# A prompt block with multi-query attention and a GELU layer on one core: when small VectorE work is issued

## The chip, the cores and the metric

The kernel runs on one core of a Trainium2 chip. The metric is device time in microseconds (us). The core's engines each run their own queue of instructions in order: TensorE (PE; its weight loads are listed apart as PEld), VectorE (DVE), ScalarE (ACT), GpSimd (POOL) and SyncE (SP), which issues the transfers.

## The reference

The input x has 2048 rows of 512 numbers, in fp32. A modulation vector is made of `c` and `w_mod` (six parts: shift, scale and gate for either half). The first half is attention, the second a GELU layer:

```
h = layernorm(x) * (1 + ca) + sa
q = h @ wq            # 32 heads of 16; k = h @ wk and v = h @ wv are shared by all heads
p = softmax(q k^T / 4)
x = x + ga * (concat_heads(p @ v) @ wo)
h = layernorm(x) * (1 + cb) + sb
x = x + gb * (gelu(h @ w1 + b1) @ w2 + b2)     # 1376 hidden numbers, tanh form
```

## The kernel before, in words

The rows are cut into 8 blocks of 256, and a block's 32 heads into 8 groups of 4 heads: 64 units, worked in order. A unit takes 8 steps over the keys, two at a time. Such a pair of steps is the kernel's rhythm. The clock that the planner counts goes up by four in it, and one count is called a tick here (the diff's words call it a half step). A pair has two halves. In each half TensorE makes four score products `e` for this unit (L650, with ScalarE's exponentials `p`, L658), four products `m` for a later unit whose row maxima VectorE takes (L527, L532), and the products of the exponentials with the values, `acc` (L675), of a step that lies behind. The products `m` share three PSUM banks.

Beside this runs the rest of the block before: output projection, second norm, GELU layer. Its products come in batches, one per pair, each cut in two halves by rows of the array (`half`, L208). A batch is taken from a queue of generators at the start of a pair. All smaller work is put off by `later(n, fn)`: `fn` is called n ticks on, and then issues its instructions on whichever engines they use, behind what stands there. So a tick sets a place in each engine's order, not a time. `due()` runs the calls whose tick has come, in the order in which they were put off: before the pair, between its halves (two ticks), and behind the second half. The order of TensorE's work follows from the generators, which ask for the tick and for what has been issued.

When a unit ends, `finish_unit` copies its sums (`oc`, L687) and sends them to memory one tick later. For blocks 5, 6 and 7 (`EARLY`) the softmax sums are then fetched as a tile of 64 x 16 (L712), inverted by VectorE (`sums`, L715) and stored (`drs`, L716); after every second head group the heads and the spread factors are fetched (`os`, L722 and L724) and GpSimd multiplies them (L728) before the norm's split (`norm_early`). The last two head groups of block 7 take another way.

`rest_steps` makes the output projection of a block in two row groups of 128 rows, t = 0 and 1. Each ends with `add_x` on VectorE (`x`, L853), bn_stats on two halves of the row (`st`, L860), and, for both groups together, bn_aggr on VectorE (`mv`, L867), four small GpSimd instructions (`ve`, `rs`, `nm`, L868 to L873) and the normed rows on GpSimd (`xh`, L880). Eight ticks after the projection TensorE may turn the normed rows (`tp`, L976 in the code, recorded at L208). Blocks 4 and 5 hold back the last 12 products of their second output sum (`w2ps`) until the next block's projection is through, so that TensorE has them during these eight ticks; the next blocks, 5 and 6, are the two that the diff's second part touches. That sum ends with `ot` on VectorE (L1083). Units 48 to 55 belong to block 6 and carry block 5's rest; units 56 to 63 carry block 6's.

Of the kernel before, what the change touches and what calls it, by code (L numbers as in the profile page):

```python
# [44 lines left out]
TAIL = (14, 9, 7)  # L45
EARLY = 5
HELD = 4
LATER = 4
LONE = 5
SOON = 6  # L50
# [13 lines left out]
def adaln_mqa_mlp(  # L64
# [24 lines left out]
    NQ = H // 4  # L89
# [67 lines left out]
    def later(n, fn):  # L157
        if draining[0]:
            fn()
        else:  # L160
            pending.append((clock[0] + n, fn))
# [518 lines left out]
    def finish_unit(u):  # L680
        b, Q = units[u]
        w = blocks[b][1]
        acc = accs.pop(u)
        if len(ocs) < 2:
            ocs.append(att.tile([P, w], F32, name=f"oc{u}", tag="oc", bufs=2))
        oc = ocs[u % 2]
        ins = nc.scalar.copy(oc, acc)  # L687
        if u - 2 in copied:
            tc.declare_no_dep(ins.ins, copied[u - 2], reason="the transfer that reads the tile's last contents comes between the two")
        copied[u] = ins.ins.name  # L690

        def send_o():
            nc.sync.dma_start(out=do[b][Q].rearrange("c r n -> (c r) n"), in_=oc)

        final = b == len(blocks) - 1
        if final and Q >= NQ - 2:
            if Q == NQ - 2:
                assert stage[b - 1] == 1
                later(2, lambda: fetch_rest(b))
                later(5, lambda: norm_early(b, range(KD - 1)))  # L700
            return
        later(1, send_o)
        if b < EARLY:
            return
        g = Q // 2
        if Q == 0:
            heads_of[b] = att.tile([P, 2, KD, w], F32, name=f"os{b}", tag="opk", bufs=1)
        os_ = heads_of[b]
        sums = wts_pool["rest"].tile([4 * w // 16, 16], F32, name=f"sums{u}", tag="sums", bufs=2)

        def fetch_sums():
            nc.sync.dma_start(out=sums, in_=do[b][Q:Q + 1, :, 16, :].rearrange("q c (t n) -> (q c) t n", n=16))  # L712

        def invert_sums():
            nc.vector.reciprocal(out=sums, in_=sums)  # L715
            nc.sync.dma_start(out=drs[b][4 * Q:4 * Q + 4, :].rearrange("h (t n) -> (h t) n", n=16), in_=sums)  # L716
            if Q % 2:
                collect()

        def collect():  # L720
            src = do[b][2 * g:2 * g + 2, :, 0:16, :].rearrange("q c r n -> (q c) r n")
            nc.sync.dma_start(out=os_[:, 0, g, :], in_=src)  # L722
            src = drs[b][8 * g:8 * g + 8, :].unsqueeze(1).to_broadcast([8, 16, w])
            nc.sync.dma_start(out=os_[:, 1, g, :], in_=src)  # L724
            later(3 if Q == NQ - 1 else 4, scale_heads)

        def scale_heads():
            nc.gpsimd.tensor_tensor(out=os_[:, 0, g, :], in0=os_[:, 0, g, :], in1=os_[:, 1, g, :], op=ALU.mult)  # L728
            if Q == NQ - 1:
                norm_early(b, [g])  # L730

        later(3, fetch_sums)
        later(4 if Q == NQ - 1 else 6, invert_sums)
        if Q == NQ - 2:
            later(5, lambda: norm_early(b, range(KD - 1)))

# [14 lines left out]
    def rest(b, fast):  # L751
# [58 lines left out]
        if b >= EARLY:  # L810
            ons[0] = on_early[b][0]
            ready[0] = clock[0] + HELD
        else:
# [19 lines left out]
    def rest_steps(b, fast, rp, bank, ons, ready):  # L833
# [4 lines left out]
        for hf in range(w // HQ):  # L838
# [20 lines left out]
            def stats(t, h):  # L859
                nc.vector.bn_stats(out=st[:, t, h, :], in_=x1[:, t, h * D // 2:(h + 1) * D // 2])  # L860
# [4 lines left out]
            def rstd(t0, t1):  # L865
                for t in range(t0, t1):
                    nc.vector.bn_aggr(out=mv[:, t, :], in_=st[:, t].rearrange("p h n -> p (h n)"))  # L867
                (nc.vector if fast else nc.gpsimd).tensor_scalar(out=ve[:, t0:t1], in0=mv[:, t0:t1, 1], scalar1=EPS,  # L868
                                                                 scalar2=0.0, op0=ALU.add, op1=ALU.add)
                nc.gpsimd.tensor_tensor(out=rs[:, t0:t1], in0=ve[:, t0:t1], in1=mhalf[:, t0:t1], op=ALU.pow)  # L870
                if not fast:
                    nc.gpsimd.tensor_tensor(out=nm[:, t0:t1], in0=mv[:, t0:t1, 0], in1=rs[:, t0:t1], op=ALU.mult)
                    nc.gpsimd.tensor_scalar(out=nm[:, t0:t1], in0=nm[:, t0:t1], scalar1=-1.0, scalar2=0.0, op0=ALU.mult, op1=ALU.add)  # L873

            def xhat(t):
                if fast:
                    nc.vector.tensor_scalar(out=xh[:, t, :], in0=x1[:, t, :], scalar1=mv[:, t, 0:1], scalar2=rs[:, t:t + 1],
                                            op0=ALU.subtract, op1=ALU.mult)
                else:
                    nc.gpsimd.tensor_scalar(out=xh[:, t, :], in0=x1[:, t, :], scalar1=rs[:, t:t + 1], scalar2=nm[:, t:t + 1],  # L880
                                            op0=ALU.mult, op1=ALU.add)
# [8 lines left out]
            def out_sum(t):  # L890
                return psum.tile([P, D], F32, name=f"wops{b}_{hf}_{t}", **bank())
# [7 lines left out]
            if fast:  # L899
                turned = [psum.tile([P, HQ], F32, name=f"turned{q}", **bank()) for q in range(2)]  # L900
                rows_o = rp.tile([P, HQ], F32, name="rows_o", tag="rb", bufs=2)
                inv = att.tile([P, H * w // P], F32, name="inv", tag="rsum", bufs=1)

                def turn_o(q):
                    for t in range(2):
                        nc.tensor.transpose(turned[q][:, t * P:(t + 1) * P], ocs[q][:, t * P:(t + 1) * P], ident)

                def scale_o(q):
                    src = turned[q].rearrange("p (t c r) -> p t c r", t=2, c=4)
                    by = inv[:, 8 * q:8 * q + 8].rearrange("p (t c) -> p t c", t=2)  # L910
                    dst = rows_o.rearrange("p (t q c r) -> p q t c r", t=2, q=2, c=4)[:, q]
                    nc.vector.reciprocal(out=by, in_=src[:, :, :, 16])
                    for t in range(2):
                        nc.vector.tensor_tensor(out=dst[:, t], in0=src[:, t, :, 0:16],
                                                in1=by[:, t].unsqueeze(2).to_broadcast([P, 4, 16]), op=ALU.mult)

                turn_o(0)
                scale_o(0)
                pss = [out_sum(t) for t in range(2)]
                yield from batches(pss[0], out_pairs(0, [0]), BATCH, end=False)  # L920
                turn_o(1)
                scale_o(1)
                yield from batches(pss[0], out_pairs(0, [1, 2]), BATCH, begin=False, end=False)
                back = psum.tile([P, HQ], F32, name="back", **bank())
                for t in range(2):
                    nc.tensor.transpose(back[:, t * P:(t + 1) * P], rows_o[:, t * P:(t + 1) * P], ident)
                split(onH[:, KD - 1, :], onL[:, KD - 1, :], back, nc.scalar, nc.vector)
                yield from batches(pss[1], out_pairs(1, [0]), BATCH, end=False)
                yield from batches(pss[0], out_pairs(0, [KD - 1]), BATCH, begin=False)
                add_out(0, pss[0])  # L930
                yield from batches(pss[1], out_pairs(1, range(1, KD)), BATCH, begin=False)
                add_out(1, pss[1])
                for t in range(2):
                    xhat(t)
            else:
                for t in range(2):
                    ps = out_sum(t)
                    yield from batches(ps, out_pairs(t, range(KD)), BATCH, lambda g: b < EARLY or g in on_early[b][1])
                    add_x(t, ps)

                    for h in range(2):
                        later(3 - 2 * t + 2 * h, lambda t=t, h=h: stats(t, h))
                projected.add(b)
            if not fast:
                later(4, lambda: rstd(0, 2))
                later(5, lambda: xhat(0))
                later(5, lambda: xhat(1))
                later(9, lambda: add_bias(0))
                later(9, lambda: add_bias(1))

                later(BUSY, lambda: state.update(busy=True))
                yield 8
# [167 lines left out]
            elif held_back:  # L1120
                yield from second(0, range(NF))
                yield from second(1, range(NF - LATER), put=add_x)
                while b + 1 not in projected:
# [525 lines left out]
```

## Time and profile before

| | |
|---|---|
| median of 3 runs | 1547.63 us (1547.52 to 1547.88) |
| the profiled execution | 1547.75 us, its span 1545.9 us |
| TensorE busy | 1531.1 us, 99% |
| VectorE busy | 1393.6 us, 90% |
| ScalarE busy | 1227.3 us, 79% |
| GpSimd busy | 671.9 us, 43% |
| granted TensorE clock | full in all 40 slices |

The busy time of TensorE is that of pipelined products, so 99% does not mean that it is at its peak. The 22 reciprocals of the softmax sums lie between 998.5 and 1468.5 us; the projection of block 5 with its norm lies around 1166 to 1206 us, that of block 6 around 1333 to 1376 us.

### The profile page before, as it was taken

How to read it: one execution, taken by the hardware profiler on the slowest of the kernel's cores; microseconds unless marked ns; L12 is line 12 of the kernel's file. 1: busy time of each engine (PE TensorE's matmuls, PEld its weight loads, DVE VectorE, ACT ScalarE, POOL GpSimd, SP SyncE). 2: the span in 40 equal slices, each digit the busy share in tenths (PEclk: the TensorE clock that was granted, in tenths of full speed). 3: DMA queues.
4: the chain of work that ended last, by engine and by line, in shares of the span. 5: the costliest groups of instructions: out<-in, count | busy, mean ns of one | idle time of the engine just before them, and what ended most of it. 6: DMA issues, size and time to landing. Idle time of an engine off the chain costs nothing.

```text
span 1545.9 us, 41617 instructions
## 1 busy us (share of the span) xinstructions
PE 1531.1 (99%) x16421; PEld 953.9 (62%) x16421; DVE 1393.6 (90%) x2487; ACT 1227.3 (79%) x2401; POOL 671.9 (43%) x1229
## 2 busy tenths in 40 slices
PE   7999999999999999999999999999999999999999
PEld 4555555567655665557655676556655676566668
DVE  7999999999999999999999999999999999999914
ACT  5677887788778887788877887788877888778874
POOL 7545422887323570246522462235711574046511
PEclk9999999999999999999999999999999999999999
DMA  9145312422030211213012120303112220203141
GB/s 294 52 138 186 118 46 79 135 74 87 23 107 17 87 57 36 94 30 99 30 56 76 56 87 23 105 25 100 57 31 73 67 96 25 88 28 98 49 151 49
DMA packets 84203, 120.85 MB, mean 78 GB/s; under 512 B 21330, under 2 KB 57426, under 8 KB 83752
## 3 DMA queue, kind: packets, MB, share of 16 engines
q1 hardware_dynamic: 84008, 118.19, 23.7%
q8 instruction: 130, 2.13, 0.6%
q14 instruction: 65, 0.53, 0.1%
HBM read 90.87 MB, written 26.74 MB: 76 GB/s over the span
## 4 chain that ended last, share of the span: by engine, by line
PE 81%; DVE 9%; issue 4%; POOL 2%; SPq 1%; DMA 1%; ACT 0%; POOLq 0%; DVEq 0%; ACTq 0%
PE acc L675 28%; PE m L527 22%; PE e L650 15%; DVE mx L532 8%; PE w1ps L208 8%; PE w2ps L208 3%; PE w2ps L197 1%; PE w1ps L197 1%; PE wops L208 1%; PE tp L208 1%; PE qps L208 1%; DMA wqf<-in_A_wq_dram 1%; SPq L498 0%; DVE st L860 0%; POOL qL L149 0%
## 5 line engine op out<-in xcount | busy, mean ns | idle before, releaser
L532 DVE TENSOR_REDUCE mx<-m 128x1 f32<-128x512 f32 x2048 | 1270.1, 682 | 82.7 <-PE m L527 59.1
L658 ACT ACTIVATE p<-e 128x512 f32<-128x512 f32 x2048 | 1097.6, 598 | 251.6 <-PE e L650 114.3
L527 PE MATMUL m<-ks,qst 64*128 64x512 f32 x2048 | 838.8, 430 | 2.1 <-DMA qst<-dq 0.7
L650 PE MATMUL e<-qst,ks 64*128 64x512 f32 x2048 | 748.9, 412 | 0.0
L675 PE MATMUL acc<-p,va 128*32 128x256 f32 x8192 | 546.8, 385 | 0.0
L527 PEld LDWEIGHTS m<-ks,qst 64*128 64x128 f32 x2048 | 367.8, 184 | 213.8 <-DVE mx L532 182.7
L650 PEld LDWEIGHTS e<-qst,ks 64*128 64x128 f32 x2048 | 363.1, 184 | 75.1 <-ACT p L658 53.4
L675 PEld LDWEIGHTS acc<-p,va 128*32 128x32 f32 x8192 | 214.5, 109 | 213.3 <-issue 108.9
L208 PE MATMUL w1ps<-h2H,w1t 64*128 64x256 f32 x1232 | 235.0, 287 | 0.0
L588 POOL TENSOR_SCALAR mt<-turned 8x32 f32<-8x32 f32 x252 | 52.7, 209 | 410.2 <-DVE turned L594 398.1
L208 PEld LDWEIGHTS w1ps<-h2H,w1t 64*128 64x128 f32 x1232 | 185.6, 184 | 29.1 <-DVE mx L532 18.5
L208 PE MATMUL w1ps<-h2L,w1t 64*128 64x256 f32 x616 | 168.9, 274 | 0.0
L208 PE MATMUL w2ps<-w2H,gH 64*128 64x512 f32 x288 | 127.1, 441 | 0.2
L208 PEld LDWEIGHTS w1ps<-h2L,w1t 64*128 64x128 f32 x616 | 113.7, 185 | 0.0
L208 PE MATMUL w2ps<-w2L,gH 64*128 64x512 f32 x288 | 112.8, 392 | 0.0
L208 PE MATMUL w2ps<-w2H,gL 64*128 64x512 f32 x288 | 112.3, 390 | 0.0
L1020 POOL TENSOR_SCALAR tt<-tt 128x256 f32<-128x256 f32 x77 | 31.2, 406 | 122.8 <-ACT tt L1019 91.4
L208 PEld LDWEIGHTS w2ps<-w2H,gH 64*128 64x128 f32 x288 | 52.9, 184 | 13.0 <-issue 2.9
L1021 POOL TENSOR_TENSOR tt<-tt,z 128x256 f32<-128x256 f32 x77 | 56.9, 739 | 6.4
L149 POOL TENSOR_TENSOR gL<-z,gH 128x256 fp32r<-128x256 f32 x77 | 56.8, 738 | 6.4
L1031 POOL TENSOR_TENSOR z<-tt,z 128x256 f32<-128x256 f32 x77 | 56.6, 735 | 6.0
L1030 POOL TENSOR_TENSOR tt<-tt,z 128x256 f32<-128x256 f32 x77 | 56.6, 735 | 0.0
(199 smaller groups left out, 1474.2 us busy)
## 6 DMA issues: line engine op xcount, KB each, us to landing
w1t<-dw SPq DMA_DIRECT2D x82, 512.0 KB
qst<-dq SPq DMA_DIRECT2D x384, 32.0 KB
do<-oc SPq DMA_DIRECT2D x62, 128.0 KB
dw<-w1s SPq DMA_DIRECT2D x11, 512.0 KB
xt<-in_A_x_dram SPq DMA_DIRECT2D x4, 1024.0 KB
dq<-qH SPq DMA_DIRECT2D x16, 256.0 KB
dq<-qL SPq DMA_DIRECT2D x16, 256.0 KB
x<-in_A_x_dram SPq DMA_DIRECT2D x8, 512.0 KB
```

The lines of the kernel that those rows point to most:

```text
L149: eng_l.tensor_tensor(out=dst_l, in0=src, in1=raw(dst_h), op=ALU.subtract)
L208: ins = nc.tensor.matmul(ps, a[rows], b_[rows], start=first_ and turn == 0, stop=last_ and turn == 1)
L527: nc.tensor.matmul(m, qsts[u][rows, j, t * P:(t + 1) * P], ks[rows, kc * 512:(kc + 1) * 512], start=True, stop=True)
L532: nc.vector.tensor_reduce(out=self.mx[u][:, i, kc:kc + 1], in_=m, axis=AX.X, op=ALU.max)
L588: nc.gpsimd.tensor_scalar(out=mt[:, g:g + 32], in0=turned[g:g + 4 * T, :], scalar1=1.0, scalar2=0.0, op0=ALU.mult, op1=ALU.add)
L650: nc.tensor.matmul(e, ks[rows, kt * P:(kt + 1) * P], rhs, start=True, stop=True)
L658: ins = nc.scalar.activation(dst, e, AF.Exp, scale=0.25)
L675: ins = nc.tensor.matmul(accs[u][32 * cidx:32 * cidx + 32, :], va[:, kt, :], rhs, start=kt == 0, stop=kt == NKT - 1)
L1020: nc.gpsimd.tensor_scalar(out=tt, in0=tt, scalar1=1.0, scalar2=1.0, op0=ALU.mult, op1=ALU.add)
L1021: nc.gpsimd.tensor_tensor(out=tt, in0=tt, in1=z, op=ALU.mult)
L1030: nc.gpsimd.tensor_tensor(out=tt, in0=tt, in1=z, op=ALU.mult)
L1031: nc.gpsimd.tensor_tensor(out=z, in0=tt, in1=z, op=ALU.add)
```

## The change

The reciprocals of the softmax sums, with all that hangs on them (store, fetch of heads and factors, GpSimd's product four ticks later), are issued ten ticks after the unit's end instead of six, except those of a block's last head group. In blocks 5 and 6 the bn_stats of the second row group are issued two ticks later, bn_aggr with GpSimd's small instructions two ticks later, and the normed rows one tick later, at the same tick as bn_aggr.

```diff
+INVERT = 10
...
         later(3, fetch_sums)
-        later(4 if Q == NQ - 1 else 6, invert_sums)
+        later(4 if Q == NQ - 1 else INVERT, invert_sums)
...
                     for h in range(2):
-                        later(3 - 2 * t + 2 * h, lambda t=t, h=h: stats(t, h))
+                        later(3 - 2 * t + 2 * h + (2 if b >= EARLY and t else 0), lambda t=t, h=h: stats(t, h))
                 projected.add(b)
             if not fast:
-                later(4, lambda: rstd(0, 2))
-                later(5, lambda: xhat(0))
-                later(5, lambda: xhat(1))
+                later(6 if b >= EARLY else 4, lambda: rstd(0, 2))
+                later(6 if b >= EARLY else 5, lambda: xhat(0))
+                later(6 if b >= EARLY else 5, lambda: xhat(1))
```

## Rows read from the trace of the kernel before

**Rows 1.** The page: busy us of each engine; a GpSimd group of the GELU.
```profile
PE 1531.1 (99%) x16421; PEld 953.9 (62%) x16421; DVE 1393.6 (90%) x2487; ACT 1227.3 (79%) x2401; POOL 671.9 (43%) x1229
...
L1031 POOL TENSOR_TENSOR z<-tt,z 128x256 f32<-128x256 f32 x77 | 56.6, 735 | 6.0
```
**Rows 2.** Waits before weight loads: total us, times, longest.
```profile
PEld m L527 <- DVE mx L532: 182.7, 468, 1.0
```
**Rows 3.** The reciprocals by tile `sums`: shortest, median, longest ns; first, last start.
```profile
L715 DVE RECIPROCAL sums<-sums x22: 233/234/245, 998.5 to 1468.5; 64x16 f32<-64x16 f32 x22
```
**Rows 4.** Half pairs of block 5's projection: length; busy us by engine, clock, DMA.
```profile
1176.75:1179.71 2.96, 2.96 (x33) 1.78 (x31) 2.96 (x6) 2.19 (x5) 0.69 (x2) 1.00 0.00 0
...
1188.22:1191.39 3.17, 3.17 (x32) 1.85 (x30) 3.17 (x6) 2.38 (x6) 0.00 (x0) 1.00 0.00 0
1191.39:1194.32 2.93, 2.93 (x31) 1.78 (x31) 2.93 (x8) 2.34 (x5) 0.86 (x2) 1.00 0.14 48
1194.32:1197.16 2.84, 2.84 (x31) 1.65 (x30) 2.62 (x6) 2.16 (x4) 2.01 (x5) 1.00 0.02 1
...
1200.01:1203.01 3.00, 2.90 (x35) 1.83 (x33) 3.00 (x6) 2.52 (x6) 2.92 (x4) 1.00 0.00 0
1203.01:1205.72 2.71, 2.71 (x35) 1.76 (x33) 2.48 (x5) 1.88 (x5) 0.23 (x1) 1.00 0.33 84
```
**Rows 5.** VectorE's time line there: start us, us, instruction, count.
```profile
1188.12 0.68 DVE L853 TENSOR_TENSOR x<-wops,x 128x512 f32<-128x512 f32 x1
...
1189.91 0.42 DVE L860 BATCH_NORM_STATS2 st<-x 128x6 f32<-128x256 f32 x1
1190.25 2.47 DVE L532 TENSOR_REDUCE mx<-m 128x1 f32<-128x512 f32 x4
1192.63 0.42 DVE L860 BATCH_NORM_STATS2 st<-x 128x6 f32<-128x256 f32 x1
...
1193.21 2.43 DVE L532 TENSOR_REDUCE mx<-m 128x1 f32<-128x512 f32 x4
...
1199.94 0.69 DVE L1083 TENSOR_TENSOR ot<-w2ps,x 128x512 f32<-128x512 f32 x1
```
**Rows 6.** TensorE's weight loads: the fourth maximum product of the half pair from 1188.22.
```profile
1190.97 0.18 PEld L527 LDWEIGHTS m<-ks,qst 64*128 64x128 f32 x1
```
**Rows 7.** Half pairs of block 6's projection, as rows 4.
```profile
1358.25:1361.53 3.28, 3.28 (x33) 1.86 (x31) 3.28 (x7) 2.51 (x6) 0.68 (x2) 1.00 0.02 4
1361.53:1364.46 2.93, 2.93 (x32) 1.80 (x31) 2.93 (x8) 1.84 (x4) 0.87 (x2) 1.00 0.01 3
...
1370.14:1373.03 2.89, 2.89 (x34) 1.83 (x32) 2.89 (x5) 2.41 (x6) 0.00 (x0) 1.00 0.23 91
```
**Rows 8.** Half pairs behind `ot`: with a reciprocal (unit 41), without (unit 17).
```profile
996.76:999.74 2.98, 2.98 (x32) 1.83 (x30) 2.98 (x6) 2.20 (x6) 0.69 (x2) 1.00 0.86 324
...
456.88:459.76 2.88, 2.88 (x32) 1.75 (x30) 2.88 (x5) 2.17 (x5) 0.68 (x2) 1.00 0.56 224
```
**Rows 9.** VectorE's time line at a reciprocal in a GELU stretch; idle time in brackets.
```profile
1450.56 0.23 DVE L715 RECIPROCAL sums<-sums 64x16 f32<-64x16 f32 x1
1450.72 2.41 DVE L532 TENSOR_REDUCE mx<-m 128x1 f32<-128x512 f32 x4
1453.43 2.48 DVE L532 TENSOR_REDUCE mx<-m 128x1 f32<-128x512 f32 x4 [0.30 <-PE m L527]
```
**Rows 10.** GpSimd's time line in block 5: first of the chain, normed rows.
```profile
1193.38 0.23 POOL L868 TENSOR_SCALAR ve<-mv 128x2 f32<-128x2 f32 x1 [15.85 <-DVE mv L867]
...
1195.07 1.53 POOL L880 TENSOR_SCALAR xh<-x,rs,nm 128x512 f32<-128x512 f32 x2
```
**Rows 11.** TensorE's first weight load for turning block 5's normed rows.
```profile
1201.31 0.18 PEld L208 LDWEIGHTS tp<-ident,xh 64*128 64x128 f32 x1
```
**Rows 12.** Waits of the SyncE queue and of GpSimd: total us, times, longest.
```profile
SPq L716 <- DVE sums L715: 57.1, 10, 6.7
...
POOL os L728 <- DMA os<-drs: 20.9, 9, 5.5
```

## The prediction, made before the change was timed

> **What bounds the kernel now.** I read the page's busy shares first: TensorE stands at 99% and VectorE at 90% of the span [rows 1], so neither share alone says which of them sets the pace. The waits say where they touch: the largest wait before TensorE's weight loads is for VectorE's maxima, 182.7 us in 468 pieces [rows 2]. Most of these 0.4 us pieces recur in every half pair and cost nothing by themselves, so the next view is the time line cut into half pairs. I cut it at the first weight load of the products with the exponentials (`acc`), which come once per half pair. An undisturbed half pair with extra products takes 2.84 to 2.85 us [the row from 1194.32 in rows 4]. It holds four maxima, which take 2.41 us from start to start of what follows (2.48 us for the merged row less the overlap, [rows 9]). So VectorE has 0.43 us to spare per half pair and TensorE paces. The half pairs that are longer than 2.85 us all have VectorE busy for their whole length: 2.96, 3.17, 2.93 and 3.00 us in block 5's projection [rows 4], 3.28 and 2.93 us in block 6's [rows 7], and 2.98 us behind an output sum with a reciprocal after it [rows 8]. These are the places where VectorE paces, and the change moves VectorE's instructions out of some of them.
>
> The mechanism is seen in [rows 5, 6]. The maxima have three PSUM banks, so the fourth maximum product of a half pair waits for the first reduction. In the half pair from 1188.22 the sum `x` ran late in the one before, a bn_stats stands in front, and the first reduction starts at 1190.25, that is 2.03 us in. The fourth product's load comes at 1190.97, 0.72 us later. The half pair is 0.33 us too long. In the next one the reduction starts 1.82 us in (1193.21) and the loss is 0.09 us. Both give one threshold: a first reduction up to about 1.73 us into the half pair costs nothing, and every later 0.1 us costs 0.1 us.
>
> **The change part by part.** *Reciprocals.* Of 22 reciprocals [rows 3], 20 move by four ticks, one pair of steps; the two after the last head group of blocks 5 and 6 stay at four ticks. Each advances VectorE by 0.16 us (1450.56 to 1450.72, [rows 9]). In none of them does VectorE wait for the sums today: they start as the reduction before them ends, and no idle time is listed before any of them. So no DMA wait is removed. What a move is worth depends on what stands in front. Behind a GELU bias or nothing, the following half pairs still have 0.30 us of idle time [rows 9], before and after the move: zero, for 14 of the 20. Two stand behind an output sum `ot`, in units 41 and 55: 2.98 us for the first, where the same place in unit 17, without a reciprocal, took 2.88 us [rows 8]; the new place has no sum in front. Gain 2 x 0.10 = 0.20 us. One stands behind block 4's second sum in a stretch without extra products, where VectorE is busy throughout on both sides of the move: between 0 and 0.16 us, I take 0, since a block of VectorE work stays as long wherever the piece stands in it. The other three are in the two held-back blocks and are counted there.
>
> What follows a reciprocal moves too: the transfer that stores it, for an odd head group the two that fetch heads and factors, and GpSimd's product of them. The SyncE queue is held up by the reciprocal today, up to 6.7 us at a time [rows 12]; behind it stand the rows of maxima, the next query tile and a weight piece. After the change the first two stand ahead of it and go out earlier; a weight piece still has three pairs (17 us) until it is read. GpSimd waits 20.9 us at its nine products [rows 12]; the wait follows the reciprocal at the same four ticks' distance, and GpSimd is 43% busy [rows 1]. In block 5's place it now comes behind both halves of the norm's transposed output instead of between them. I set all this at zero, with a bound of 0.3 us either way. After the maxima have run out (last reciprocal) VectorE is idle: zero.
>
> *Block 5, second row group and norm.* Half pair by half pair, from [rows 4, 5] and the threshold:
> - 1176.75 (2.96): its reciprocal goes, the reduction starts 0.16 us earlier, below the threshold. Gain 0.11.
> - Two half pairs on, the reciprocal joins the first group's second bn_stats: 0.34 + 0.16 us in front, with VectorE free about 1.2 us in; the first reduction starts at about 1.68. Just below the threshold: zero, by 0.05 us.
> - 1188.22 (3.17): no bn_stats any more; the start goes from 2.03 to 1.69. Gain 0.33.
> - 1191.39 (2.93): one bn_stats (0.34) instead of bn_stats and two bn_aggr (0.58, 1192.63 to 1193.21). Start about 1.60. Gain 0.09.
> - 1194.32 (2.84): the other bn_stats and the bn_aggr arrive, 0.58 us. Start about 1.75. Cost 0.02.
> - The next one has the turned maxima in front and the held-back sum `ot` of 0.69 us, as before, but with some 0.2 us of backlog. It still just fits: cost 0.01.
> - 1200.01 (3.00; an undisturbed one with transposes takes 2.71): the reciprocal goes (-0.16), the backlog replaces it (+0.17). Cost 0.01 to 0.02.
> Gain 0.11 + 0.33 + 0.09 - 0.05 = 0.48 us.
>
> *Block 6.* [rows 7] 1358.25 (3.28): reciprocal and bn_stats go, 0.44 gained. 1361.53 (2.93): 0.09 gained. The one after, an ordinary one now, gets bn_stats, reciprocal and bn_aggr together, 0.34 + 0.16 + 0.24 = 0.74 us; the first reduction starts 1.92 us in: cost 0.19. The one with `ot` and its follower stay. Gain 0.34 us.
>
> *The cover of the later norm.* Against the transposes, bn_aggr ends 2.8 us later in block 5 (1.75 us into the half pair from 1194.32 instead of 1.82 us into the one from 1191.39) and 3.0 us later in block 6; GpSimd then needs 3.2 us until the normed rows are there (1193.38 to 1196.60, [rows 10]). The transposes read them at 1201.31 [rows 11]: 4.7 us to spare now, 1.7 to 1.9 us left. If that were gone, the transposes would wait, and TensorE with them.
>
> Sum: 0.20 + 0.48 + 0.34 = 1.0 us. The profiled execution took 1547.75 us (span 1545.9, the rest around it); that is 0.12 us above the median of the three runs. Taken from the median: 1547.63 - 1.0 = **1546.6 us**.
>
> [...]
>
> **The rivals.**
> 1. *The bunch only moves.* Block 6's new 0.74 us bunch and the sums behind it keep a backlog longer than my threshold allows, and block 5's does too. For: in both, the bunch lands one half pair ahead of `ot`, and two of my starts lie within 0.05 us of the threshold. Against: the bunch is no longer right behind a sum of 0.6 us. If each bunch still costs what it costs now, 1547.4 to 1547.6.
> 2. *All of it goes.* VectorE catches up before each bunch, and the stalls of [rows 4, 7, 8] vanish: 0.11 + 0.33 + 0.09 + 0.29 + 0.44 + 0.09 + 0.18 + 0.2 = 1.7 us, so 1545.9. Against: `ot` alone costs 0.04 us in [rows 8], and it stays.
> 3. *The normed rows come too late* (the slower side). GpSimd's chain starts behind a later bn_aggr; if it slips by more than the 1.7 to 1.9 us left, the two blocks' transposes wait. A slip of a whole half pair in each is 2 x 2.85 = 5.7 us less the 1.0: 1552.3. Against: nothing else stands in GpSimd's queue between the turned maxima and the chain [rows 10].
> 4. *Moved reciprocals are held by GpSimd.* In the GELU stretches each would wait for a GpSimd instruction of 0.735 us [rows 1]. It decides from a wait of 0.33 us on, where wait and reciprocal (0.16) exceed the 0.30 us of idle time and the 0.19 us up to the threshold; at the full 0.735 us that is 0.4 us each, some 12 times: 1546.6 + 4.8 = 1551.4. Against: the 22 reciprocals took 233 to 245 ns, and the ones that already lie beside GELU are as short as the rest [rows 3, 9]. [...]
>
> That the edit would not do what it says is excluded: the order of TensorE's work does not hang on the moved calls, so only VectorE's, GpSimd's and SyncE's orders change.
>
> **How the numbers follow.** Forecast 72%, within 0.5 us of 1546.6. Rival 1: 13%. Rival 2: 9%. Rival 3: 4%. Rival 4: 2%. A measurement of this kernel can tell about 0.2% (3.1 us) from no change; the forecast and the first two rivals lie inside, all stalls that the change touches add up to 1.7 us. So within 0.2%: 93%; slower: 4% (part of rivals 3 and 4 is too small to be told); faster: 3%, for something the trace does not show. The range takes rival 1 with 0.3 us for the unknown transfers, and rival 2 with as much: 1545.4 to 1548.0.
>
> **What would show it.** Right: the half pairs that answer to 3.17 and 3.28 us take 2.84 to 2.9; the one behind block 6's now about 3.03; those behind `ot` 2.88 instead of 2.98; the reciprocals still 0.23 us without idle time before them; the transposes do not wait for GpSimd. Wrong: new half pairs over 2.9 us where the reciprocals arrive among GELU work, TensorE's transposes waiting for the normed rows, or a difference of more than 2 us that sits outside the stretches named here.

## The result, and the profile after

The changed kernel took 1550.62 us (median of 17 runs, 1549.61 to 1554.21) against 1547.87 us for the kernel before on the same chips: a ratio of 1.0018, with a 95% interval of 1.0011 to 1.0026. That is 1.7 to 4.0 us slower, where 1.0 us faster was forecast, with a range that ended at 1548.0. The profiled execution has a span of 1548.3 us. Its single runs also scatter more widely (4.6 us) than those of before (2.9 us); the four longest of them, from 1551.75 us on, are the four whose mean granted clock was 0.998 or 0.999, and the other 13, at 1.000, lie between 1549.61 and 1551.67 us.

The half pairs of the changed kernel, cut in the same way as [rows 4, 7, 8], show both what went as forecast and what did not. Columns as there: stretch, length, then busy time by engine.

```profile
997.12:1000.00 2.88, 2.88 (x32) 1.73 (x30) 2.88 (x5) 2.17 (x5) 0.67 (x2) 1.00 0.96 364
1077.98:1081.10 3.12, 3.07 (x38) 2.05 (x36) 2.75 (x5) 2.79 (x7) 2.96 (x5) 1.00 0.64 236
1188.70:1191.56 2.86, 2.86 (x33) 1.67 (x31) 2.86 (x5) 2.17 (x4) 0.00 (x0) 1.00 0.00 0
1191.56:1194.40 2.84, 2.84 (x32) 1.69 (x30) 2.84 (x7) 2.49 (x6) 0.00 (x0) 1.00 0.14 49
1194.40:1197.23 2.83, 2.83 (x32) 1.68 (x30) 2.83 (x8) 2.16 (x5) 0.91 (x2) 1.00 0.02 1
...
1200.08:1202.99 2.91, 2.90 (x34) 1.83 (x32) 2.91 (x5) 2.43 (x6) 2.68 (x6) 1.00 0.24 91
1259.06:1262.89 3.83, 3.11 (x39) 2.08 (x37) 3.47 (x6) 2.80 (x7) 3.18 (x5) 1.00 0.63 230
1359.19:1362.04 2.85, 2.85 (x32) 1.67 (x30) 2.85 (x5) 2.17 (x5) 0.68 (x2) 1.00 0.01 1
1364.88:1367.78 2.90, 2.90 (x32) 1.77 (x30) 2.90 (x8) 2.19 (x5) 0.86 (x2) 1.00 0.16 44
1395.42:1399.31 3.89, 3.09 (x38) 2.05 (x36) 3.52 (x7) 2.80 (x7) 1.84 (x3) 1.00 0.42 139
1442.05:1446.19 4.14, 3.07 (x38) 2.06 (x36) 3.49 (x6) 2.78 (x7) 3.17 (x5) 1.00 0.27 101
```

The stretches that the change aimed at are shorter: 3.17 became 2.86 us, 2.93 became 2.84, 3.00 became 2.91 [rows 4], 3.28 became 2.85 [rows 7], 2.98 became 2.88 [rows 8]. Pair by pair, measured at the starts of the exponentials, the two traces differ there by 1.3 us in favour of the change. But four pairs that the prediction did not touch are longer: the first pairs of units 45, 53, 59 and 61 take 0.27, 0.97, 1.05 and 1.29 us more, 3.6 us together. They are the half pairs of 3.12, 3.83, 3.89 and 4.14 us above, all in the GELU stretch, in the unit behind one in whose last pair heads and factors are fetched. There no engine is busy for the whole length: something waits. Before, the same half pair of unit 53 took 2.87 us, with TensorE busy throughout:

```profile
1259.14:1262.01 2.87, 2.87 (x42) 2.04 (x44) 2.50 (x5) 2.74 (x6) 2.47 (x4) 1.00 0.96 369
```

(Between the two spans lie also 0.5 us less in the tail, which all eight later profiles show in the same size whatever was edited, 0.1 us in the start-up, and about half a microsecond more, spread in hundredths over the other pairs.)

ScalarE's time line in the long half pair at unit 53 shows which wait: the tanh of the GELU stands between the exponentials, waits 0.94 us for GpSimd, and the exponentials stand behind it.

```profile
1257.98 2.27 ACT L659 ACTIVATE p<-e 128x512 f32<-128x512 f32 x4 [0.27 <-PE e L651]
1260.20 0.37 ACT L688 COPY oc<-acc 128x256 f32<-128x256 f32 x1
1261.51 0.42 ACT L1025 ACTIVATE tt<-tt 128x256 f32<-128x256 f32 x1 [0.94 <-POOL tt L1022]
1261.83 2.25 ACT L659 ACTIVATE p<-e 128x512 f32<-128x512 f32 x4
```

Over the whole run the tanh waits for GpSimd four times, 3.4 us together (total, times, longest), which is nearly all of the 3.6 us:

```profile
ACT tt L1025 <- POOL tt L1022: 3.4, 4, 1.3
```

GpSimd's time line there: the product of heads and factors (L729; L728 before) waits 3.40 us for its transfer, and the two GELU instructions that the tanh needs (L1021, L1022) stand behind the product, though they have nothing to do with it.

```profile
1259.55 0.73 POOL L729 TENSOR_TENSOR os<-os 128x256 f32<-128x256 f32 x1 [3.40 <-DMA os<-drs]
1260.25 0.41 POOL L1021 TENSOR_SCALAR tt<-tt 128x256 f32<-128x256 f32 x1
1260.74 0.74 POOL L1022 TENSOR_TENSOR tt<-tt,z 128x256 f32<-128x256 f32 x1
```

Over the whole run GpSimd waits 51.4 us at this product, where it waited 20.9 us before [rows 12]. Only the four waits with GELU work behind them cost time. The longest, at the fetch in unit 54, has the norm's split behind it, and no pair there is longer:

```profile
POOL os L729 <- DMA os<-drs: 51.4, 10, 12.2
```

And TensorE's own weight load of the next `e` product waits for ScalarE to free a bank:

```profile
1262.46 0.18 PEld L651 LDWEIGHTS e<-qst,ks 64*128 64x128 f32 x1 [0.93 <-ACT p L659]
```

Why the transfer lands later stands in SyncE's queue. Before, the store of the inverted sums went out 0.26 us after the reciprocal, which started at 1246.40, and the product could start at 1251.80, 5.40 us after the reciprocal:

```profile
1246.40 0.23 DVE L715 RECIPROCAL sums<-sums 64x16 f32<-64x16 f32 x1
1246.66 0.51 SPq L716 DMA_DIRECT2D drs<-sums  x1
1247.22 0.64 SPq L722 DMA_DIRECT2D os<-do  x1
1248.36 0.60 SPq L724 DMA_DIRECT2D os<-drs  x1
```

After, the reciprocal starts at 1252.05, but the eight transfers of the next query tile stand in front of the store. It goes out 1.56 us after the reciprocal, and the product starts 7.50 us after it:

```profile
1252.05 0.23 DVE L716 RECIPROCAL sums<-sums 64x16 f32<-64x16 f32 x1
...
1248.83 1.87 SPq L499 DMA_DIRECT2D qst<-dq  x3
1250.74 0.44 SPq L501 DMA_DIRECT2D qst<-dz  x1
1251.22 1.81 SPq L499 DMA_DIRECT2D qst<-dq  x3
1253.07 0.43 SPq L501 DMA_DIRECT2D qst<-dz  x1
1253.61 0.86 SPq L717 DMA_DIRECT2D drs<-sums  x1
1254.51 0.65 SPq L723 DMA_DIRECT2D os<-do  x1
1255.67 0.63 SPq L725 DMA_DIRECT2D os<-drs  x1
1256.39 0.88 SPq L822 DMA_DIRECT2D w1t<-dw  x2
```

So 2.10 us were added: 1.30 in SyncE's queue, 0.36 between the store's issue and the fetch's, 0.44 from the fetch's issue to the product.

The kernel before had too little room for that. In its GpSimd and ScalarE lines at the same fetch, where the product comes one pair earlier, the GELU product that the tanh needs ended at 1253.72 and the tanh started at 1254.47, 0.75 us later:

```profile
1251.80 0.74 POOL L728 TENSOR_TENSOR os<-os 128x256 f32<-128x256 f32 x1 [1.10 <-DMA os<-drs]
...
1252.99 0.73 POOL L1021 TENSOR_TENSOR tt<-tt,z 128x256 f32<-128x256 f32 x1
```
```profile
1252.32 2.27 ACT L658 ACTIVATE p<-e 128x512 f32<-128x512 f32 x4 [0.27 <-PE e L650]
1254.47 0.42 ACT L1024 ACTIVATE tt<-tt 128x256 f32<-128x256 f32 x1
...
1258.01 2.27 ACT L658 ACTIVATE p<-e 128x512 f32<-128x512 f32 x4 [0.28 <-PE e L650]
...
1260.50 0.42 ACT L1024 ACTIVATE tt<-tt 128x256 f32<-128x256 f32 x1
...
1436.25 0.42 ACT L1024 ACTIVATE tt<-tt 128x256 f32<-128x256 f32 x1 [0.29 <-POOL tt L1021]
```

The tanh of the next pair, the first of unit 53, starts a little later in its pair, since the copy `oc` stands in front of it there: 2.49 us behind the pair's first exponential (1258.01 to 1260.50) instead of 2.15 us (1252.32 to 1254.47). So the change's product, which comes in that pair, has a margin of 0.75 + 0.34 = 1.09 us. The last line, at the fetch in unit 60, shows a wait that was already there before the change, 0.29 us long; there was no margin, and the pair behind this fetch lost most (1.29 us). Both could have been read before the prediction.

### The profile page after: what moved, and what is told of

Read it like the earlier page. It is cut to its first block, busy times and chain, and to the rows that moved or that the text cites. A ratio compares the mean times of both kernels' runs of the same rounds, so it can differ in the third digit from the quotient of the medians.

```text
span 1548.3 us, 41624 instructions
## 1 busy us (share of the span) xinstructions
PE 1531.1 (99%) x16421; PEld 953.8 (62%) x16421; DVE 1394.4 (90%) x2487; ACT 1227.7 (79%) x2401; POOL 671.8 (43%) x1229
## 4 chain that ended last, share of the span: by engine, by line
PE 87%; DVE 10%; ACT 1%; DMA 1%; POOL 0%; issue 0%; SPq 0%; DVEq 0%; POOLq 0%; ACTq 0%
PE acc L676 30%; PE m L528 25%; PE e L651 15%; DVE mx L533 8%; PE w1ps L209 7%; PE w2ps L209 4%; PE w2ps L198 1%; PE w1ps L198 1%; PE wops L209 1%; PE tp L209 1%; PE qps L209 1%; DVE st L861 0%; PE modr L293 0%; DVE x L854 0%; PE wops L198 0%
## 5 line engine op out<-in xcount | busy, mean ns | idle before, releaser
L1021 POOL TENSOR_SCALAR tt<-tt 128x256 f32<-128x256 f32 x77 | 31.2, 405 | 112.8 <-ACT tt L1020 86.4
L1022 POOL TENSOR_TENSOR tt<-tt,z 128x256 f32<-128x256 f32 x77 | 56.9, 739 | 6.4
L1032 POOL TENSOR_TENSOR z<-tt,z 128x256 f32<-128x256 f32 x77 | 56.6, 735 | 6.0
```

The source lines that it names most:

```text
L1021: nc.gpsimd.tensor_scalar(out=tt, in0=tt, scalar1=1.0, scalar2=1.0, op0=ALU.mult, op1=ALU.add)
L1022: nc.gpsimd.tensor_tensor(out=tt, in0=tt, in1=z, op=ALU.mult)
L1032: nc.gpsimd.tensor_tensor(out=z, in0=tt, in1=z, op=ALU.add)
```

## The experiments

Theory T: the moved transfers land later; GpSimd's product waits for them; GELU work stands behind the product; ScalarE waits for that work with the exponentials behind it. Rivals: R1, the reciprocals among GELU work hold up VectorE; R2, weight pieces come late behind the moved transfers; R3, the norm comes too late for the transposes. Every kernel ran beside the kernel before on the same chip; "pairs" are measured at the starts of the exponentials in its trace, against those of the kernel before.

**The two parts apart.** The second part alone:

```diff
-INVERT = 10
+INVERT = 6
```

> Second part of the change alone: the reciprocals stay at six ticks, statistics of the second row group and the norm go later. Theory T (the moved reciprocals make the fetch of the softmax factors land later; GpSimd's product waits for it, GELU's small work stands behind the product, ScalarE's tanh waits for that, and the exponentials stand behind the tanh): none of that is here, so the half pairs behind the second sums gain 0.33 + 0.09 us in block 5 and about 0.3 + 0.09 us in block 6, and some 0.3 us come back behind the held-back output sum: 0.5 us below the kernel before. Rival R3 (the norm now comes too late for the transposes): as slow as the change, 2 to 3 us above the kernel before.

Measured: 1546.66 us, where the kernel before took 1547.62 us on that chip (as for the next three kernels), ratio 0.9990 (0.9981 to 0.9999). The pairs of [rows 4] and [rows 7] are 0.40 and 0.43 us shorter and no other pair is longer but the very first, in which the granted clock stood at 0.50 for 3.41 us from 72.84. R3 falls. The 0.3 us that were to come back behind the held-back sum did not: that half pair is 3.00 us, as before.

The first part alone:

```diff
-                        later(3 - 2 * t + 2 * h + (2 if b >= EARLY and t else 0), lambda t=t, h=h: stats(t, h))
+                        later(3 - 2 * t + 2 * h, lambda t=t, h=h: stats(t, h))
...
-                later(6 if b >= EARLY else 4, lambda: rstd(0, 2))
+                later(4, lambda: rstd(0, 2))
```
(and the normed rows at five ticks again)

> First part of the change alone: reciprocals at ten ticks, statistics and norm as before. Theory T: the four long pairs of the changed kernel (first pairs of units 45, 53, 59, 61; together 3.6 us more than before) are here again, less about 0.6 us gained where the reciprocals stood behind sums: 2.5 to 3.5 us above the kernel before, and single runs scattered over some us, as with the change. R3: no slower than before, since the norm is where it was.

Measured: 1552.19 us (1550.43 to 1553.20), ratio 1.0026 (1.0016 to 1.0036): the loss is the first part's. It is 4.6 us, more than the 2.5 to 3.5 us expected: the four pairs are longer by 0.87, 1.30, 0.90 and 1.89 us, 5.0 us together and not 3.6. The chain from reciprocal to product took 7.40, 7.83, 7.47 and 8.44 us at these places, against 6.82, 7.50, 7.61 and 7.83 us in the change: 0.58, 0.33, -0.14 and 0.61 us more. The pairs lost 0.60, 0.33, -0.15 and 0.60 us more. So with the margin used up the chain's delay is paid in full; why the chain is longer here is not shown. ScalarE's waits (total, times, longest) have the tanh's four:

```profile
ACT tt L1025 <- POOL tt L1022: 4.8, 4, 1.9
```

**The product moved out of the way.** Reciprocals, transfers and their order as in the change:

```diff
-            later(3 if Q == NQ - 1 else 4, scale_heads)
+            later(3 if Q == NQ - 1 else 8, scale_heads)
```

> The whole change, but GpSimd's product of heads and factors is issued eight ticks after the reciprocal instead of four; reciprocals, transfers and their order in SyncE's queue are those of the changed kernel. Theory T: the factors have landed when GpSimd comes to the product, the idle time before it is 0 to 0.5 us in the GELU stretches, the tanh waits for nothing, the four long pairs are 5.7 us again, and the gains of the change are left: 1 us below the kernel before. Rival R1 (reciprocals in the midst of GELU work hold up VectorE and through it TensorE) and rival R2 (weight pieces stand behind the moved transfers and come late): the long pairs stay, 2 to 3 us above the kernel before.

Measured: 1546.17 us (1545.86 to 1547.69), ratio 0.9990 (0.9981 to 0.9999). None of the four pairs is long, and all gains of the change are there. GpSimd's line in unit 53 has the GELU work first and the product without idle time:

```profile
1258.49 0.74 POOL L1022 TENSOR_TENSOR tt<-tt,z 128x256 f32<-128x256 f32 x1
...
1262.01 0.73 POOL L729 TENSOR_TENSOR os<-os 128x256 f32<-128x256 f32 x1
```

R1 and R2 fall: VectorE's order and SyncE's are those of the change.

**The query tile moved out of the way.** The product stays at four ticks:

```diff
-                if self.left[u] == size[u] // 2 and u > 1 and u + 1 < NU:
+                if self.left[u] == size[u] // 2 - (4 if units[u][0] >= EARLY else 0) and u > 1 and u + 1 < NU:
                     load_q(u + 1)
```

> The whole change, but from block 5 on the next query tile is fetched four maxima later, so that its eight transfers stand behind the factors' transfers in SyncE's queue and not in front of them. GpSimd's product stays at four ticks. If the wait in T is long because the moved transfers stand behind the query tile (about 1.3 us in the queue and some more in flight), the idle time before the product falls from 3.4 and 3.7 us to about 1.5 to 2 us at units 53 and 61, and the long pairs go or shrink below 0.3 us: 0.5 to 1 us below the kernel before, if the query tile is still in time for the maxima. If the product is simply four ticks too near to the work behind it, whatever the queue, the long pairs stay at 1 us. R1 and R2: 2 to 3 us above the kernel before.

Measured: 1546.33 us, ratio 0.9988 (0.9979 to 0.9997); none of the four pairs is long. SyncE's queue has the store 0.27 us after the reciprocal (1252.21):

```profile
1252.48 0.51 SPq L717 DMA_DIRECT2D drs<-sums  x1
1253.03 0.65 SPq L723 DMA_DIRECT2D os<-do  x1
1255.07 0.61 SPq L725 DMA_DIRECT2D os<-drs  x1
```
and GpSimd comes to the product 5.89 us after the reciprocal, with half the idle time:

```profile
1258.10 0.74 POOL L729 TENSOR_TENSOR os<-os 128x256 f32<-128x256 f32 x1 [1.78 <-DMA os<-drs]
```

So the position in SyncE's queue, not the four ticks as such, is what made the wait too long. The product still waits, but not long enough to reach the tanh.

**Transfers late, reciprocals where they were.**

```diff
+            if Q == NQ - 1:
+                store_sums()
+            else:
+                later(4, store_sums)
+
+        def store_sums():
             nc.sync.dma_start(out=drs[b][4 * Q:4 * Q + 4, :].rearrange("h (t n) -> (h t) n", n=16), in_=sums)
```
(with the reciprocal at six ticks again, the fetch of heads and factors behind the store, and statistics and norm as before)

> The kernel before with the reciprocals where they were on VectorE, six ticks after the unit's end, and with statistics and norm where they were; only the store of the inverted sums and the fetch of heads and factors are issued at ten ticks, with GpSimd's product four ticks behind them. Theory T: the transfers stand behind the query tile in SyncE's queue as with the change, the factors land as late, and the four long pairs are there (3.5 to 5 us together): 3 to 5 us above the kernel before. Rival R1 (VectorE's reciprocals in the midst of GELU work are the cost): no slower than the kernel before, since VectorE's order is that of before.

Measured: 1553.80 us (1550.32 to 1555.41), where the kernel before took 1547.33 us on that chip (as for the next kernel), ratio 1.0039 (1.0026 to 1.0051). The four pairs are longer by 1.16, 0.82, 1.04 and 1.69 us, 4.7 us together, as expected. The time is 6.5 us above the kernel before and not 3 to 5. In the profiled execution, the one of 1555.41 us, 3.4 us of the difference lie ahead of the second pair of unit 0, where the granted clock stood at 0.50 twice for 3.42 us:

```profile
33.32:36.74 3.42, 3.42 (x10) 2.68 (x9) 3.32 (x4) 1.28 (x2) 3.42 (x4) 0.50 0.94 289
74.28:77.70 3.42, 3.42 (x26) 1.87 (x26) 2.54 (x5) 0.97 (x2) 0.00 (x0) 0.50 0.00 0
```

That part is not the edit's; the lowest run lies 3.0 us above the kernel before. VectorE's order is that of before, so VectorE has no part in the loss.

**The last link.** The wait of GpSimd left as it is, the tanh one tick later:

```diff
-                later(3 if fast else 4, tanh)
+                later(3 if fast else 5 if b >= EARLY - 1 else 4, tanh)
```

> The whole change, but from block 4's rest on the GELU's tanh is issued one tick later, behind the second half of its pair instead of between the halves. Reciprocals, transfers and GpSimd's product are those of the changed kernel. Theory T: GpSimd still waits some 3.4 to 3.7 us at units 53 and 61 and 9 us at unit 59, but ScalarE has 2.84 us more before it comes to the tanh, so the tanh waits for nothing, and the four long pairs are gone: 0.7 to 1.5 us below the kernel before. If the exponentials are held up by something other than the tanh in front of them, the long pairs stay: 2 to 3 us above it.

Measured: 1548.54 us, ratio 1.0004 (0.9995 to 1.0013). Half a hit: units 53 and 59 are as before, but 45 and 61 stay 0.56 and 1.16 us longer, so the gain that was expected did not come. The tanh waits for nothing now, but the next GELU's square does. Its tile `tt` has two buffers, and GpSimd still has to read the old contents (`z`, L1032), behind the same product. ScalarE in unit 61:

```profile
1444.63 0.42 ACT L1025 ACTIVATE tt<-tt 128x256 f32<-128x256 f32 x1
1446.15 0.42 ACT L1020 ACTIVATE tt<-z 128x256 f32<-128x256 f32 x1 [1.09 <-POOL z L1032]
1446.47 2.25 ACT L659 ACTIVATE p<-e 128x512 f32<-128x512 f32 x4
```

T had named the tanh alone. In its wider form it says that whatever ScalarE needs from GpSimd behind the product will do. The next kernel adds to this one:

```diff
-                tt = rp.tile([P, HQ], F32, name=f"tt{b}_{hf}_{f}", tag="h322" if odd else "tt", bufs=2)
+                tt = rp.tile([P, HQ], F32, name=f"tt{b}_{hf}_{f}", tag="h322" if odd or (not fast and b >= EARLY - 1 and f % 4 > 1) else "tt", bufs=2)
```

> The kernel of e5_tanh_later (the whole change, tanh one tick later), and the GELU's tile tt takes turns among four buffers instead of two from block 4's rest on. In e5_tanh_later two long pairs were left, units 45 (+0.56 us) and 61 (+1.16 us); there ScalarE waits 1.1 us with the square of the GELU, whose tile GpSimd still reads behind its late product. Theory T in its wider form (whatever ScalarE needs from GpSimd behind the late product holds up the exponentials): with four buffers that wait is gone too, and no long pair is left although GpSimd waits as long as before: 0.7 to 1.5 us below the kernel before. If the square waited for something else, the two long pairs stay: within 0.5 us of e5_tanh_later.

Measured: 1546.64 us, where the kernel before took 1548.36 us on that chip, ratio 0.9988 (0.9979 to 0.9997). No long pair is left, although GpSimd waits 4.46 us at unit 53, longer than in the change:

```profile
1263.35 0.75 POOL L729 TENSOR_TENSOR os<-os 128x256 f32<-128x256 f32 x1 [4.46 <-DMA os<-drs]
```

GpSimd's idle time itself cost nothing here; it cost where another engine's queue came to its result.

**Both remedies together** (the edits of e3 and e4):

> The whole change with both remedies: GpSimd's product eight ticks after the reciprocal, and the next query tile fetched four maxima later from block 5 on. Theory T: either remedy alone took away all four long pairs, so both together give no more: within 0.3 us of either, 1.0 to 1.6 us below the kernel before; the idle time before the product is zero in the GELU stretches. If small waits had been left by the single remedies, up to 0.5 us more would go.

Measured: 1546.21 us (1545.64 to 1547.18), ratio 0.9993 (0.9984 to 1.0002), on a chip where the kernel before took 1547.33 us: no more than either alone. Which of e1, e3, e4, e6 and e8 is best can't be told; their intervals overlap. e1, e3, e4 and e8 are clear of the kernel before and of the change.

## Why the prediction was wrong, point by point

- **The failed step** is in the paragraph on what follows a reciprocal: "I set all this at zero, with a bound of 0.3 us either way." Its reasons did not carry. "[T]he wait follows the reciprocal at the same four ticks' distance" counts ticks, and a tick orders each engine's queue but says nothing of a transfer's time: the chain from reciprocal to product grew from 5.40 to 7.50 us. "GpSimd is 43% busy" is an average, and what mattered was the margin of 1.09 us between GpSimd's result and ScalarE's tanh in that pair. The right price is the chain's growth less that margin, 2.10 - 1.09 = 1.01 us, and 0.97 us was measured there. At unit 45 the same working gives 1.62 - 1.32 = 0.30 us (0.27 measured), at unit 61, without a margin, 1.31 us (1.29 measured). The four places together made 3.6 us. (GpSimd's "nine products" are eleven; nine of them waited. The sum does not hang on it.)
- The SyncE queue was looked at from one side. The prediction says that the rows of maxima and the query tile "go out earlier", which is true (the query tile at 1248.83 instead of 1252.14), but what moves ahead holds back what it passes (the store, by 1.30 us). The weight piece was checked for being late; the transfer that had moved was not. The same queue has another such hold: behind the store, the factors' fetch, which needs what the store writes, waits 0.4 us for it and is issued 2.06 us after it (1253.61 to 1255.67), and the weight piece behind the fetch, for which no wait of its own is listed, goes out only then (1256.39).
- Block 5: forecast 0.48 us. The half pairs of 2.96, 3.17 and 2.93 us lost 0.10, 0.31 and 0.09, and the 3.00 one lost 0.09 where I had it 0.02 longer: the bunch of 0.58 us left no backlog. Mechanism right, 0.1 us too careful.
- Block 6: forecast 0.34 us. 3.28 became 2.85 as said; the bunch of 0.74 us cost 0.06 us (2.90) and not 0.19. The threshold of 1.73 us holds; the start was misjudged. The half pair began at 1364.88 and its first reduction started at 1366.67, 1.79 us in and not 1.92.

```profile
1366.67 2.43 DVE L533 TENSOR_REDUCE mx<-m 128x1 f32<-128x512 f32 x4
```

- Reciprocals behind `ot`: 0.10 us each, as forecast (2.98 to 2.88). The one in block 4's plain stretch: 0.13 us gained in one pair and 0.12 lost in the next, zero as assumed.
- The later norm: `xh` ends at 1199.46 and the transposes start at 1201.39, 1.93 us to spare; 1.7 to 1.9 were forecast. Rival 3 was wrong for the reason given.

```profile
1196.24 0.23 POOL L869 TENSOR_SCALAR ve<-mv 128x2 f32<-128x2 f32 x1 [18.16 <-DVE mv L868]
...
1197.93 1.53 POOL L881 TENSOR_SCALAR xh<-x,rs,nm 128x512 f32<-128x512 f32 x2
```

- Rival 4: the reciprocals still take 233 to 244 ns, without idle time before them. Nothing holds them.

```profile
L716 DVE RECIPROCAL sums<-sums x22: 233/235/244, 1003.9 to 1475.2; 64x16 f32<-64x16 f32 x22
```

- None of the rivals was the one that happened. Its engine, its wait (20.9 us at the product, [rows 12]) and its queue were all on the page; they were dismissed with an average. Rival 2 was nearer than it looked: the part of the sum that VectorE's places made up came out at 1.3 us, between the 1.0 us forecast and its 1.7 us.

What stays open: whether the transfers' landing times add to the scatter of single runs is not shown. The 0.5 us in the tail, by which the profile of before differs from all others, was not followed up.

## What to carry to other kernels

Where an instruction is moved that starts a transfer, follow the transfer to the instruction that waits for it, then what stands behind that one in its queue, and then the first reader of that on another engine; the price is the delay less the margin found on this way, at the place where the moved work will stand. Count queue positions in time, not in ticks: what a moved transfer lets pass is issued before it. A product that waits for memory is best placed where the rest of its queue has just been served, as in e3, and not in front of small work that the busy engines take up next.

## What the runs showed of the hardware that was not expected

Two dependent transfers through memory (4 KB out, 128 KB back) took 5.1 us from the store's issue to the start of the product in the kernel before (1246.66 to 1251.80) and 5.9 us right behind the query tile's transfers (1253.61 to 1259.55); in e4, without these in front, 5.6 us. The first share of the 2.10 us is queueing in SyncE; the rest, up to 0.8 us, varies from place to place. The fetch of the factors, which waits for the store, was issued 1.70 to 1.76 us behind it at all eleven places of the kernel before, and 1.69 to 3.01 us behind it in the change.
